# A fused attention and gated MLP on one core: one pair fetched per period, Erf behind the mean at a group's end, and means by two one-pass products

## The chip, the core and the metric

The kernel runs on one core of a Trainium2 chip. The metric is the device time of one execution, in microseconds (us). The engines are called as in the profile: PE is TensorE's matmuls and PEld its weight loads, DVE is VectorE, ACT is ScalarE, POOL is GpSimd, and SP is SyncE, which only issues transfers here.

## What is computed

The reference, cut to what matters (8 batches, 8 heads, 576 positions, 64 values per head; the MLP has 4608 rows, 512 in and out, 2048 hidden):

```python
kv = np.einsum('bhsd,bhse->bhde', k, v)            # per head, 64 x 64
out = np.einsum('bhsd,bhde->bhse', q, kv)
rms = np.sqrt(np.mean(out * out, axis=-1, keepdims=True) + 1e-06)
x = (out / rms * g_norm)                           # then (B,H,S,D) -> (B*S, H*D)

h = x @ w_in                                       # 4608 x 512 @ 512 x 2048
sp = np.maximum(h, 0.0) + np.log1p(np.exp(-np.abs(h)))
g = h * erf(sp)
return g @ w_out
```

## The kernel before

**Groups.** The rows are worked in nine groups of 512. Groups 0 to 7 are the first 512 positions of each batch, and group 8 (T == B in the code) collects the 64 positions left over of all eight batches. While the MLP of group T runs, the attention of group T + 1 is made, in four pairs of heads (p = 0 to 3).

**Number formats.** Group 0, the first two hidden tiles of group 1 and most of group 1's output layer multiply in fp32 (L907 for the hidden layer, L727 for the output). Elsewhere every factor is cut into forms of which each is multiplied in one pass: a high form, a low form, and one that combines both (`thirds`, with `upper` on ACT, L609, and `lower` on DVE, L612 and L615). A product of 128 x 512 then is twelve one-pass matmuls (L671): eight into the bank `n_ps`, four into `m_ps`. ACT empties `n_ps` (L1057) and DVE adds `m_ps` (L649). Six PSUM banks are used in turn as three pairs, so that a product needs the banks of the third product before it.

**Periods.** Groups 2 to 8 run in periods of a quarter of the hidden layer (four tiles of 128; the loop over m from L1007). A period has four hidden products (`hidden`), one after the other, with Softplus on each (L1072), then Erf on the four in two halves (L1078), then the four results (`result`, j = 0 to 3) of the period before. The gates `h * s` are multiplied on DVE (L1101), and the gated h is cut in its turn at the start of the next period.

**Attention of a pair, in pieces.** For groups 3 to 7 (`fused`) they are: `visit` (it multiplies q by kv, and turns q and makes k^T v for the pair after it), `halve` (the squares cut into a high and a low half, L521 and L522), `keep_tail` (copies out of PSUM), `loads` (the fetches of q, k and v of a later pair), `mean` (the products with the averaging matrix, L537 and L538 for halves or L543 in fp32, then Ln, Exp and Square on ACT, L552 to L554), `norm` (three DVE steps, L560 to L572) and `split` (into x's three forms). Mean squares are made in fp32 in groups 0, 1 and 8 and by halves in the others. `places` says behind which hidden product or result of the period a piece is put: at the last period of a group (b == NB - 1) `mean` is at place 5, behind the first result and behind Erf, `norm` at 6 and `split` at 7. A pair ahead of that is kept by `prepare` and `keep_prepared` in groups 1 and 2, whose pieces are put into the steps of groups 0 and 1 by `pieces_of`.

**What sets the order.** Each engine works through its own list in the order in which the code writes it. q, k and v of a pair lie in two buffers of each kind (`kvp`); the sync queue issues the fetches of pairs, the weights' parts (L809) and the stores in one order. Functions of ScalarE come in sets; a change of set is a table load (L105 for Ln and Exp, L108 for Softplus, L1078 for Erf's).

The lines that put the fetches in place, before:

```python
def loads():
    if not fused or (T, p) == (FIRST + 1, 0):
        load_pair(T * NP + p + 2)
    if fused:
        load_pair(T * NP + p + 3)
```

Of the kernel before, what the change touches and what calls it, by code (L numbers as in the profile page):

```python
# [54 lines left out]
FIRST = 2  # L55
# [5 lines left out]
def kernel(  # L61
# [10 lines left out]
    nc = tc.nc  # L72
# [320 lines left out]
    def keep_prepared():  # L393
        kept.pop()()

    def attention(T, p, pools=None):

        st = {}

        halves = FIRST <= T < B  # L400
        quad = 0 < T < B
        fused = FIRST < T < B
        then = divmod(T * NP + p + 1, NP)
# [55 lines left out]
        def visit():  # L459


            qT, tail = ready.pop((T, p))
            at = st["at"] = at_tile()
            x = halves_of(qT)
            for a, i, o in ((0, 0, 0), (0, 1, 1), (1, 0, 1), (1, 1, 0)):
                nc.tensor.matmul(  # L466
                    at[rows_of[o], a, 0 : 2 * P],
                    lhsT=bd[rows_of[i], a * D : a * D + D],
                    rhs=x[rows_of[i], a],
                    start=True,  # L470
                    stop=True,
                )
            for s in rows_of:
                nc.tensor.matmul(
                    at[s, 0, 2 * P : 2 * P + R], lhsT=bd[s, 0:D], rhs=tail[s], start=True, stop=True
                )
            st["o"] = at[:, :, 0 : 2 * P]
            st["next"] = fused and then[0] < B
            if st["next"]:
                ps = pair_of_banks("q0_ps", "q1_ps")  # L480
                kvs = list(kv_products(*then, at, crossed=True))
                turns = list(turn_products(*then, ps))
                while kvs or turns:
                    for some in (turns, kvs):
                        for product_ in some[:4]:
                            product_()  # L486
                        del some[:4]
            if fused:
                st["sq"] = x_new.tile([P, G], FP32, name="sq", tag="x")
            else:  # L490
                st["sq"] = qT
            nc.scalar.activation(two(st["sq"]), st["o"], AF.Square)
            if st["next"]:
                qT = turned(*then, ps)
                tails_kept(*then, ps, qT)

        def keep_tail():
            nc.vector.tensor_copy(
                out=x_last[:, p, T * R : T * R + R], in_=st["at"][:, 0, 2 * P : 2 * P + R]
            )  # L500
            if st["next"]:
                kv_kept(*then, st["at"])

        def apply():
# [53 lines left out]
        def norm():  # L558
# [19 lines left out]
                op1=ALU.mult,  # L578
            )

        def split():
            if T >= FIRST:
                thirds(st.pop("x"), *(form[:, p] for form in x_forms[T]))

        def loads():
            if not fused or (T, p) == (FIRST + 1, 0):
                load_pair(T * NP + p + 2)
            if fused:
                load_pair(T * NP + p + 3)

        if T == 0:
            return products, apply, halve, mean, norm
        if T == B:
            return lambda: None, square, lambda: None, mean, norm, split

        prepare_ = partial(prepare, T, p)
        if fused:
# [3 lines left out]
            pieces = ((prepare_,), (visit,), (halve, keep_tail, loads))  # L601
        else:
            pieces = ((prepare_, loads), (visit,), (keep_tail,))
        return (*(partial(chain, *group) for group in pieces), mean, norm, split)


    def upper(x, high):
# [20 lines left out]
    def thirds(x, high, low, both):  # L628
        upper(x, high)
        lower(x, high, low, both)  # L630
# [182 lines left out]
    def pieces_of(T):  # L813


        steps = [([], [], []) for _ in range(FC)]
        for p in range(NP):
            products, apply, halve, mean, norm, split = attention(T, p)
            f = (BATCH - 1) * (p + 1) if T < FIRST else BATCH * p

            steps[f][2 if T == FIRST or p == 1 else 1].append(products)
            steps[f + 1][0].append(keep_prepared)
            steps[f + 1][1].append(apply)
            steps[f + 2][0].append(halve)
            with_erf = (f + 2) % BATCH == BATCH - 1

            place = 2 if T < FIRST and p == 0 else 1
            steps[f + 2][place].append(partial(mean, table=not with_erf))
            steps[f + 3][0].append(norm)
            steps[min(f + 4, FC - 1)][0].append(split)  # L830
        return steps
# [27 lines left out]
    for n in range(FIRST * FC + 1):  # L859
# [10 lines left out]
        if T < FIRST:  # L870
            if f == 0:
                steps = pieces_of(T + 1)

            if due(0 if n == 2 * (BATCH - 1) else 1):
                weights()
            for key in list(w_new)[:2]:
                w_lower(*key)
            for piece in steps[f][0]:
                piece()
# [127 lines left out]
    for m in range(first_batch, batches + 1):  # L1007
        T, b = divmod(m, NB)
        todo = []
        if T + 1 < NG:  # L1010
            todo = list(attention(T + 1, b))
            if b == 0:
                side = late_r if T % 2 == FIRST % 2 else late
                forms = side.tile([P, 3, KC, G], FP32R, name=f"x_forms{(T + 1) % 2}")
                x_forms[T + 1] = [forms[:, i] for i in range(3)]

        def piece():
            if todo:
                todo.pop(0)()


        places = (0, 2, 3, 5, 6, 8)
        if T + 1 == B:
            places = (0, 0, 0, 5, 6, 7)
            if b == NB - 1:


                places, todo[3] = (0, 0, 0, 4, 6, 7), partial(todo[3], table=False)
                todo[5] = partial(chain, todo[5], softplus_table)
        elif b == NB - 1:  # L1030
            places = (0, 2, 3, 5, 6, 7)

        def pieces(place):
            while todo and places[-len(todo)] <= place:
                todo.pop(0)()

        def fetch(place):
            for which in FETCH[place].split():
                load_parts(which, 1)


        to_last = m == B * NB - 1
        pieces(0)
        g, done = g_next, len(g_next)
        g_next = []
        if m < batches:

            pool, tag = (acc, "e") if m % 2 else (wide, "b")
            h = pool.tile([P, BATCH, G], FP32, name="h", tag=tag)
            s = gate_r.tile([P, BATCH, G], FP32, name="s", tag="s")  # L1050
        for i in range(BATCH):
            if m < batches:
                n_ps, m_ps = hidden(T, b * BATCH + i)
            fetch(i)

            def evacuate():
                nc.scalar.activation(h[:, i], n_ps, AF.Copy, scale=SHIFT - 1.0)  # L1057
                add(h[:, i], m_ps)


            early_copy = i == 0 and m == B * NB
            if early_copy:
                evacuate()
            if i == 0:
                for half in range(done, 2):
                    g.append(cut_upper(old_h, half))
            if i == 0 and not done:
                cut_lower(old_h, 0, g[0])
            if m < batches:
                if not early_copy:  # L1070
                    evacuate()
                nc.scalar.activation(s[:, i], h[:, i], AF.Softplus)  # L1072
            if i == BATCH - 1:
                cut_lower(old_h, 1, g[1])
            pieces(i + 1)
        if m < batches:
            for i in range(2):
                nc.scalar.activation(part(s, i), part(s, i), AF.Erf)  # L1078
            if len(todo) < 2:
                softplus_table()  # L1080
        T2, b2 = divmod(m - 1, NB)
        w = [w_now["out", b2 * BATCH + f].pop(0).bitcast(FP32R) for f in range(BATCH)]
        for j in range(J):
            cuts = 2 if m == batches and j == J - 1 else 1
            result(T2, b2, j, g, w, cuts)
            fetch(BATCH + j)
            if b2 == NB - 1:
                e = es.pop(j)
                if cuts == 1:
                    store(T2, j, e)  # L1090
            if j == 1 and m == batches - 1:
                cut_lower(h, 0, g_next[0])

            if m >= batches - 1:
                due_halves = (j,) if j < 2 and m < batches else ()
            else:
                due_halves = range(2) if j == (2 if to_last else 1) else ()
            if to_last:
                pieces(BATCH + 1 + j)
            for half in due_halves:  # L1100
                nc.vector.tensor_tensor(  # L1101
                    out=part(h, half), in0=part(h, half), in1=part(s, half), op=ALU.mult
                )
            if j == 0 and m == batches - 1:
                g_next.append(cut_upper(h, 0))
            pieces(BATCH + 1 + j)
        old_h = h
# [33 lines left out]
```

## Time and profile before

| | before |
|---|---|
| time, median of 3 runs | 943.47 us (943.17 to 945.06) |
| span of the profiled execution | 943.4 us |
| granted TensorE clock, mean | 0.998 of full speed |
| PE busy | 920.1 us, 98% |
| DVE busy | 728.8 us, 77% |
| ACT busy | 603.1 us, 64% |
| DMA, mean over the span | 275 to 276 GB/s |
| groups 0 and 1 (to the first product of group 2) | about 254 us |
| one of groups 3 to 6 | about 98.7 us, four periods |

Busy shares are means over stages with different limits. A matmul's record reaches from its start to the modelled end of its pipeline, so that neighbouring records overlap and a busy PE isn't yet one at its peak. What a stage is bound by is read from the waits and from the spacing of its instructions. In a row of the timeline the first number is the start and the second the length in us; an idle stretch ahead and what ended it stand in brackets. Pieces of the chain of waits are start, us, what.

### The profile page before, as it was taken

What the parts mean: (1) busy time and instruction counts of PE and PEld (TensorE: products, weight loads), DVE (VectorE), ACT (ScalarE), POOL (GpSimd) and SP (SyncE); (2) the same over time, 40 slices, a digit from 0 to 9 for tenths busy, and PEclk for the clock granted to TensorE, in tenths of its full rate; (3) what the DMA queues carried; (4) which work ended last, traced back from release to release, by engine and by line L of the source; (5) the groups of instructions that cost most, each with busy time, mean ns of one, the idle gap of its engine ahead of it and who ended that gap; (6) DMA issues with size and microseconds to landing.
All of it is one profiled execution on the core that took longest, in us unless ns stands there. A gap on an engine that the chain in (4) does not pass through costs nothing.

```text
span 943.4 us, 15388 instructions
## 1 busy us (share of the span) xinstructions
PE 920.1 (98%) x5998; PEld 685.3 (73%) x5998; DVE 728.8 (77%) x1074; ACT 603.1 (64%) x830; POOL 2.4 (0%) x10
## 2 busy tenths in 40 slices
PE   6999999999999999999999999999999999999998
PEld 4444445565687887888788878887888788888886
DVE  2788848788576888888878887888888878776677
ACT  3877666677665666666656666666666666665552
POOL 1000000000000000000000000000000000000000
PEclk9999999999999999999999999999999999999999
DMA  9866406888589998899888988998877678778872
GB/s 258 287 209 205 135 1 253 322 342 333 200 288 333 330 335 296 289 321 329 272 296 311 320 290 303 333 309 278 284 318 261 247 264 342 275 281 324 321 271 56
DMA packets 108271, 259.99 MB, mean 276 GB/s; under 512 B 43992, under 2 KB 66856, under 8 KB 108200
## 3 DMA queue, kind: packets, MB, share of 16 engines
q1 hardware_dynamic: 106488, 256.73, 76.8%
q10 hardware_dynamic: 1648, 2.29, 0.8%
q8 instruction: 47, 0.77, 0.3%
q14 instruction: 24, 0.20, 0.1%
q0 software_dynamic: 64, 0.00, 0.0%
HBM read 224.40 MB, written 34.60 MB: 275 GB/s over the span
## 4 chain that ended last, share of the span: by engine, by line
PE 71%; DVE 16%; ACT 6%; DMA 4%; issue 2%; SPq 0%; DVEq 0%; ACTq 0%
PE n_ps L671 35%; PE m_ps L671 17%; PE o_ps L727 8%; PE h_ps L907 4%; DVE e L649 3%; DVE h L1101 2%; DVE e L644 2%; DVE h L649 2%; PE at_ps L466 1%; DVE g_forms L612 1%; DMA w_in_parts<-w_in 1%; PE at_ps L486 1%; DMA k_sb<-in_k_dram 1%; DVE x L572 1%; DVE u L563 1%
## 5 line engine op out<-in xcount | busy, mean ns | idle before, releaser
L671 PE MATMUL n_ps<-x_forms,w_in_parts 128*128 128x512 f32 x896 | 227.8, 395 | 6.2 <-DVE x_forms L612 3.9
L671 PE MATMUL n_ps<-w_out_parts,g_forms 128*128 128x512 f32 x928 | 232.0, 392 | 0.0
L671 PEld LDWEIGHTS n_ps<-w_out_parts,g_forms 128*128 128x128 f32 x928 | 172.9, 188 | 37.1 <-issue 1.9
L671 PEld LDWEIGHTS n_ps<-x_forms,w_in_parts 128*128 128x128 f32 x896 | 167.1, 188 | 45.0 <-DVE x_forms L612 5.6
L1072 ACT ACTIVATE s<-h 128x512 f32<-128x512 f32 x112 | 70.8, 632 | 190.4 <-DVE h L649 190.3
L649 DVE TENSOR_TENSOR h<-m_ps,h 128x512 f32<-128x512 f32 x116 | 79.9, 689 | 90.8 <-ACT h L1057 60.3
L671 PE MATMUL m_ps<-w_out_parts,g_forms 128*128 128x512 f32 (+1 forms) x468 | 124.3, 388 | 0.0
L671 PE MATMUL m_ps<-x_forms,w_in_parts 128*128 128x512 f32 x448 | 120.5, 391 | 0.0
L727 PE MATMUL o_ps<-w_out_sb,h_sb 128*128 128x512 f32 x224 | 101.8, 597 | 0.2 <-DVE h_sb L857 0.2
L671 PEld LDWEIGHTS m_ps<-w_out_parts,g_forms 128*128 128x128 f32 x468 | 87.5, 188 | 18.5
L671 PEld LDWEIGHTS m_ps<-x_forms,w_in_parts 128*128 128x128 f32 x448 | 84.7, 189 | 17.8
L649 DVE TENSOR_TENSOR e<-m_ps,e 128x512 f32<-128x512 f32 (+1 forms) x117 | 80.3, 687 | 14.5 <-PE m_ps L671 3.8
L727 PEld LDWEIGHTS o_ps<-w_out_sb,h_sb 128*128 128x128 f32 x224 | 41.4, 190 | 44.8 <-issue 42.2
L1057 ACT ACTIVATE h<-n_ps 128x512 f32<-128x512 f32 x112 | 66.1, 590 | 10.4 <-PE n_ps L671 10.2
L615 DVE SCALAR_TENSOR_TENSOR g_forms<-g_forms 128x1024 fp32r<-128x1024 f32 x58 | 71.1, 1225 | 2.0
L612 DVE TENSOR_TENSOR g_forms<-h,g_forms 128x1024 fp32r<-128x1024 f32 x58 | 70.5, 1216 | 0.1
L609 ACT ACTIVATE g_forms<-h 128x1024 fp32r<-128x1024 f32 x58 | 58.4, 1048 | 15.1 <-PE m_ps L671 11.1
L1101 DVE TENSOR_TENSOR h<-h,s 128x1024 f32<-128x1024 f32 x56 | 65.9, 1216 | 0.0
L907 PE MATMUL h_ps<-xT,w_in_sb 128*128 128x512 f32 x144 | 64.8, 596 | 0.5 <-DVE w_in_sb L245 0.5
L644 DVE SCALAR_TENSOR_TENSOR e<-n_ps,e 128x512 f32<-128x512 f32 x88 | 60.1, 683 | 3.5 <-PE n_ps L671 3.5
L108 ACT ACT_TABLE_LOAD x44 | 56.5, 1283 | 0.7
L1078 ACT ACTIVATE s<-s 128x1024 f32<-128x1024 f32 x56 | 56.3, 1053 | 0.3
(128 smaller groups left out, 1023.4 us busy)
## 6 DMA issues: line engine op xcount, KB each, us to landing
w_out_parts<-w_out SPq DMA_DIRECT2D x116, 768.0 KB
w_in_parts<-w_in SPq DMA_DIRECT2D x112, 768.0 KB
w_in<-w_new SPq DMA_DIRECT2D x16, 768.0 KB
q_sb<-in_q_dram SPq DMA_DIRECT2D x32, 256.0 KB
w_raw<-in_moe_w_in_dram SPq DMA_DIRECT2D x16, 512.0 KB
w_raw<-in_moe_w_out_dram SPq DMA_DIRECT2D x8, 1024.0 KB
out_dram<-e SPq DMA_DIRECT2D x32, 256.0 KB
k_sb<-in_k_dram SPq DMA_DIRECT2D x28, 287.5 KB
```

Of the source, the lines that this page charges most:

```text
L108: nc.scalar.preload_act_table_set("softplus")
L609: nc.scalar.activation(high, x, AF.Copy, scale=1.0 + 2.0**-13)
L612: nc.vector.tensor_tensor(out=low, in0=x, in1=high.bitcast(FP32), op=ALU.subtract)
L615: nc.vector.scalar_tensor_tensor(out=both, in0=low.bitcast(FP32), scalar=SHIFT, in1=high.bitcast(FP32), op0=ALU.mult, op1=ALU.add,)
L644: nc.vector.scalar_tensor_tensor(out=out_, in0=ps, scalar=scale, in1=out_, op0=ALU.mult, op1=ALU.add)
L649: nc.vector.tensor_tensor(out=out_, in0=ps, in1=out_, op=ALU.add)
L671: nc.tensor.matmul(ps[:, cols], lhsT=weights(form, k), rhs=moving(form, k)[:, cols], start=(form == forms[0] and k == 0), stop=(form == fo ...
L727: nc.tensor.matmul(o_ps[j], lhsT=g[:, j * P : j * P + P], rhs=w_out_sb[:, f, :], start=(f == 0), stop=last,)
L907: nc.tensor.matmul(plain[i], lhsT=w_in_sb[:, i % FC, c], rhs=xT[T][:, c, :], start=(c == 0), stop=(c == KC - 1),)
L1057: nc.scalar.activation(h[:, i], n_ps, AF.Copy, scale=SHIFT - 1.0)
L1072: nc.scalar.activation(s[:, i], h[:, i], AF.Softplus)
L1101: nc.vector.tensor_tensor(out=part(h, half), in0=part(h, half), in1=part(s, half), op=ALU.mult)
```

## The change

There are four edits, and none changes what is computed but for the rounding of the mean squares in two groups.

- **Fetches.** Every period fetches one pair, the second after its own. Before, the first fused period fetched two pairs and each later one the third after its own. For group 1 the fetches move from the step of `prepare` to the step of `keep_tail`.
- **The end of groups 2 to 6** (`turn`). The mean is put at place 4, behind the last hidden product, with its ACT steps ahead of Erf; norm and high form follow the first result, the low forms the second; Erf of the second half comes behind the first result; the gates move from the second to the third result. At the start of each group from 3 to 8 the first hidden product is copied out of PSUM ahead of the cut of the gated h (`early_copy`; before, in group 8 alone).
- **k^T v's copy.** In groups 0 and 1 `keep_prepared` runs at the top of a step, ahead of the weight cuts. In the fused visits the tails of the next pair are copied behind the halves.
- **Means.** Groups 1 and 8 cut the squares into halves and multiply these in one pass each.

```diff
-        halves = FIRST <= T < B
+        halves = 0 < T
...
             if st["next"]:
-                qT = turned(*then, ps)
-                tails_kept(*then, ps, qT)
+                st["turned"] = ps, turned(*then, ps)
...
-            if st["next"]:
+            if st.get("next"):
+                tails_kept(*then, *st.pop("turned"))
                 kv_kept(*then, st["at"])
...
+        def split_upper():
+            if T >= FIRST:
+                upper(st["x"], x_forms[T][0][:, p])
+
+        def split_lower():
+            if T >= FIRST:
+                lower(st.pop("x"), *(form[:, p] for form in x_forms[T]))
...
         def loads():
-            if not fused or (T, p) == (FIRST + 1, 0):
-                load_pair(T * NP + p + 2)
-            if fused:
-                load_pair(T * NP + p + 3)
+            load_pair(T * NP + p + 2)
...
         if T == B:
-            return lambda: None, square, lambda: None, mean, norm, split
+            return lambda: None, square, halve, mean, norm, split
...
-            steps[f + 1][0].append(keep_prepared)
             steps[f + 1][1].append(apply)
...
                 weights()
+            while kept:
+                keep_prepared()
             for key in list(w_new)[:2]:
                 w_lower(*key)
...
+        turn = b == NB - 1 and T + 1 < B
         if T + 1 < NG:
-            todo = list(attention(T + 1, b))
+            todo = list(attention(T + 1, b, in_parts=turn))
...
-        elif b == NB - 1:
-            places = (0, 2, 3, 5, 6, 7)
+        elif turn:
+            places, todo[3] = (0, 2, 3, 4, 5, 5, 6), partial(todo[3], table=False)
...
-            early_copy = i == 0 and m == B * NB
+            early_copy = i == 0 and b == 0 and first_batch < m < batches
...
-            for i in range(2):
+            for i in range(1 if turn else 2):
                 nc.scalar.activation(part(s, i), part(s, i), AF.Erf)
...
-                due_halves = range(2) if j == (2 if to_last else 1) else ()
-            if to_last:
+                due_halves = range(2) if j == (2 if to_last or turn else 1) else ()
+            if to_last or turn:
                 pieces(BATCH + 1 + j)
+            if turn and j == 0:
+                nc.scalar.activation(part(s, 1), part(s, 1), AF.Erf)
+                softplus_table()
```

More of the change, by code (lines that the diff above doesn't have):

```diff
@@ L394, in keep_prepared, with attention @@
         kept.pop()()
-    def attention(T, p, pools=None):
+    def attention(T, p, pools=None, in_parts=False):
         st = {}
-        halves = FIRST <= T < B
+        halves = 0 < T
         quad = 0 < T < B
@@ L579, in norm @@
             )
+        def split_upper():
[4 more added lines that the diff above has]
+                lower(st.pop("x"), *(form[:, p] for form in x_forms[T]))
         def split():
-            if T >= FIRST:
-                thirds(st.pop("x"), *(form[:, p] for form in x_forms[T]))
+            split_upper()
+            split_lower()
         def loads():
-            if not fused or (T, p) == (FIRST + 1, 0):
-                load_pair(T * NP + p + 2)
-            if fused:
-                load_pair(T * NP + p + 3)
+            load_pair(T * NP + p + 2)
         if T == 0:
@@ L603, in attention @@
             pieces = ((prepare_, loads), (visit,), (keep_tail,))
-        return (*(partial(chain, *group) for group in pieces), mean, norm, split)
+        after = (split_upper, split_lower) if in_parts else (split,)
+        return (*(partial(chain, *group) for group in pieces), mean, norm, *after)
     def upper(x, high):
```

## The prediction

> **What bounds the kernel now.** I read the page first, then the waits of TensorE (PE, and PEld for its weight loads), then the chain of waits and the timeline around each of these waits.
>
> ```profile
> PE 920.1 (98%) x5998; PEld 685.3 (73%) x5998; DVE 728.8 (77%) x1074; ACT 603.1 (64%) x830; POOL 2.4 (0%) x10
> ...
> PE 71%; DVE 16%; ACT 6%; DMA 4%; issue 2%; SPq 0%; DVEq 0%; ACTq 0%
> ```
>
> TensorE sets the pace: 71% of the chain. The 98% flatter it, since matmuls overlap; the pace is the spacing of the weight loads. A product of 12 one-pass matmuls takes 2.72 us from one product's first load to the next one's (352.43 to 355.15). What can be won is therefore TensorE's own work and the stretches in which this spacing breaks.
>
> ```profile
> PEld n_ps L671 <- DVE x_forms L612: 5.6, 5, 1.1
> ...
> PE n_ps L671 <- DMA w_in_parts<-w_in: 1.9, 1, 1.9
> ...
> PE at_ps L466 <- DVE bd_kv L364: 1.6, 1, 1.6
> ```
>
> Columns: us in total, times, longest. Three waits, and each has its own part in the change. The first comes at the start of a group. Its timeline:
>
> ```profile
> 453.38 1.32 PEld L671 LDWEIGHTS n_ps<-x_forms,w_in_parts 128*128 128x128 f32 x6
> ...
> 456.44 0.19 PEld L671 LDWEIGHTS n_ps<-x_forms,w_in_parts 128*128 128x128 f32 x1 [1.14 <-DVE x_forms L612]
> 456.55 0.90 PEld L671 LDWEIGHTS m_ps<-x_forms,w_in_parts 128*128 128x128 f32 x4
> 457.50 1.81 PEld L671 LDWEIGHTS n_ps<-x_forms,w_in_parts 128*128 128x128 f32 x8
> ```
>
> The first product of the group takes 457.50 - 453.38 = 4.12 us in place of 2.72. The low form of the last pair of x came late. Why, the chain of waits tells:
>
> ```profile
> 450.02 2.27 DVE h L1101 x2
> 452.29 0.61 DVE u L560
> 452.92 0.70 DVE u L563
> 453.65 0.75 DVE x L572
> ...
> 455.79 0.61 DVE x_forms L612
> ...
> 456.44 0.50 PE n_ps L671
> ```
>
> The gates (L1101) stand ahead of the norm in DVE's order, and a result's two additions between the norm and the split.
>
> The second wait stands alone, just after the main part begins; chain of waits again, then a row of the busy time by stretch:
>
> ```profile
> 270.32 8.44 DMA k_sb<-in_k_dram
> ...
> 279.26 11.45 DMA w_in_parts<-w_in
> 290.70 0.14 issue
> 290.84 3.14 PE n_ps L671 x8
> ```
>
> ```profile
> 291.60:295.00 3.40, 3.40 (x9) 2.65 (x8) 0.00 (x0) 1.22 (x2) 0.00 (x0) 0.50 1.06 407
> ```
>
> Weights fetched at 279.26 land at 290.70, behind the second of two pairs fetched in that period (its k was issued at 270.32). The 0.50 is the granted clock: after the stall TensorE runs at half speed for 3.4 us.
>
> **What the Trainium skill says.** "TensorE: Matmul & The Clock Gate", What's actually happening: the clock halves after an idle window of about 3.4 us and needs a busy one to come back. The 3.4 us at 0.50 agree; the loads stood only 2.32 us here, less than a window, and there the trace decides. The same page, Architectural detail: VectorE and ScalarE are strictly first in, first out. The chain above shows it: what stands ahead is waited for. "FP8 and Floating Point Precision", TensorE Precision Notes: true fp32 takes four passes. The trace has a 512-column fp32 product as two records, 0.86 us in all, against 0.226 us for a one-pass matmul: 3.8 times. "ScalarE: Activation LUTs", What ACT_TABLE_LOAD costs: about 1283 ns for every set; the trace has 1283 (L105, L108).
>
> **The change, part by part.**
>
> *One pair per period.* Each period after the first now fetches the next pair but one where it fetched the third; in all as many bytes. What goes is the second fetch at 269.6 to 275.9: 832 KB, at the 417 GB/s of 288.00 to 291.60 an estimated 2.0 us of transfer, and 6.4 us in which the sync queue held back the fetches behind it. The weights are due at 288.7, where TensorE would have begun, and landed at 290.7, so even the 2.0 us alone just suffice. Won: the product before the stall, 285.92 to 290.81, 4.89 - 2.72 = 2.17, and the one at half clock, 290.81 to 295.03, 4.22 - 2.72 = 1.50. Sum 3.7 us; at least 2. The shorter lead: a pair issued around 462 is read by the visit of the next period, near 485; the longest landing in the chain is 11.45 us. Hidden.
>
> *Group end.* In five periods (those that end groups 2 to 6) the mean's products go ahead of the first result, Ln, Exp and Square ahead of Erf, norm and split ahead of the gates. Table loads stay three. From the stamps of 440 to 458: Softplus ends at 445.5; table 1.28, Ln 0.69, Exp 0.63, Square 0.63: u at 448.8 (before: 452.2). DVE is free of the first result's additions at 448.6; norm 0.68 + 0.69 + 0.75 gives x at 451.0; ScalarE's high form 451.8, between the two Erfs (1.28 + 1.05 end at 451.1); the second result's additions to 452.4; low 453.1, both 453.8. TensorE wants high at 454.7, low at 455.0: no wait. The five first products took 3.62, 4.12, 4.11, 4.08 and 4.21 us: 20.14 - 5 x 2.72 = 6.5 us.
> The price: gates run at 455.2 to 457.5 where they ran at 449.9 to 452.3, and the last result's additions end at 458.9. Behind these in DVE's queue wait the new group's first addition and the cut of the gated h. The visit's banks must be free at 459.4 (0.5 us to spare), the third product wants the first one's bank at 460.5 and gets it at 459.6, because the early copy lets ScalarE empty it ahead of the cut. The fourth has 0.6 to spare. Group 7 has no visit, so there the third product comes 0.2 us too early. I take 6.3; both ends 3 and 6.9.
>
> *k^T v's copy.* In groups 0 and 1 it moves ahead of up to two weight cuts, 4 x 0.69 = 2.75 us. One visit waits: from n_ps at 170.8 to o_ps at 176.56 are 5.75 us, against 3.66 for the same stretch at 200.68. Two us are too much to count, for DVE is full there (11.71 of 12 us) and the next mean then waits for its halves, ready at 181.1 where TensorE could start at 180.8. I take 1.7, from 1.2 to 2.1. In the fused visits the tail copies move behind the halves: the mean's input comes about 0.5 us sooner, off the path.
>
> *Means of groups 1 and 8.*
>
> ```profile
> L522 DVE TENSOR_TENSOR sq_lo<-sq,sq_hi 128x512 fp32r<-128x512 f32 x20 | 13.8, 692 | 0.7
> ...
> L521 DVE CAST sq_hi<-sq 128x512 fp32r<-128x512 f32 x20 | 8.4, 422 | 13.0 <-ACT sq L492 13.0
> ...
> L543 PE MATMUL at_ps<-qT,mean_w 128*128 128x256 f32 x16 | 4.1, 379 | 0.0
> ...
> L543 PE MATMUL ms_ps<-sq,mean_w 128*128 128x512 f32 x8 | 4.1, 592 | 0.0
> ```
>
> Rows of the groups of instructions (busy us, mean ns): L543 on at_ps is group 1's mean, on ms_ps<-sq group 8's; L521 and L522 cut a square into halves.
>
> An fp32 mean holds TensorE 0.86 us in group 1 (chain, 75.45) and 0.89 in group 8 (828.98 to 829.43, and the n_ps after it 0.44 over its 1.81); by halves, 0.47 (four times 0.12, at 182.93) and 2 x 0.226. Saved 0.39 and 0.44 a pair. Added to DVE 0.42 + 0.69 = 1.11 us a pair. In group 8 it lies in DVE's gap before the period's first addition: 4 x 0.44 = 1.7 won. In group 1 three pairs have slack (the halves can be ready at 71.1, the mean comes at 75.3): 3 x 0.39 = 1.2. The first pair has none: from the square's end at 51.57 DVE's weight join runs to 55.67 and h_ps waits for it, so 1.1 are lost there. That group's fetches come two steps later, with four steps of about 7.8 us left: hidden.
>
> Sum: 3.7 + 6.3 + 1.7 + 1.7 + 1.2 - 1.1 = 13.5 us. 943.5 - 13.5 = **930.0 us**.
>
> **Rivals.**
> - The group end's wait comes back as a bank or DVE wait. For it: DVE has 77%, and the gates come 5 us later. Against: every margin above is positive. All of it lost: 936.3; half: 933.
> - The weights are late all the same, since the DMA share is 1.0 there: 930.0 + 3.7 = 933.7. Against: 2.0 to 6.4 us of room.
> - The halves of group 1 delay the weight joins in each of four pairs, no gain from the copy: 930.0 + 3 x 1.1 + 1.7 = 935.0. Against: one h_ps wait for a join after 40 us in the whole trace.
> - Slower: pairs fetched one period ahead come late. If each of the 19 visits of groups 3 to 7 that prepare another one waits 1 us and half of these drop the clock for 3.4 us (1.5 each), 19 + 14 = 33 are lost: 963. Against: 22 us of room.
>
> **How the numbers follow.** Forecast (within 2.5 of 930) 0.68, the first rival 0.12, second 0.07, third 0.05, slower 0.04, the parts cancelling 0.04. The three middle rivals are still faster by over 0.2% (1.9 us), so faster 0.92, same 0.04, slower 0.04. Range: all upper ends together (3.7 + 6.9 + 2.1 + 2.9, no loss) give 927.9, and a little more for spacing that the rows don't show, 926.5; above, the first rival at its worst, 936.5.
>
> **What would show it.** The five waits for x_forms gone and each group 2.72 us to its second product; no 0.50 clock near 292; the visit near 173 starting without a wait; L543 left with group 0 alone; a w_in_sb wait near 56 of 1 us more. Wrong would be: visits waiting for k_sb or v_sb, PE waiting on h or e (L649) after a group's start, or the weights' wait merely moved.

## The result and the profile after

| | before | after |
|---|---|---|
| time, median | 944.03 us (943.17 to 945.06, 4 runs) | 935.99 us (934.74 to 937.02, 4 runs) |
| span and time of the profiled execution | 943.4, 945.18 us | 935.2, 937.02 us |
| start of group 2's first product | 253.88 us | 255.95 us |
| from there to the end of the span | 689.5 us | 679.3 us |

The ratio after to before is 0.9914, with a 95% interval of 0.9894 to 0.9933: 8.0 us won, where 13.5 were forecast. The spans of the two profiles are 8.2 us apart. The last two rows say where to look: the periods of groups 2 to 8 gave 10.2 us, and groups 0 and 1 with their steps took 2.1 back.

The page after, its rows of busy time and of the chain of waits:

```profile
PE 916.1 (98%) x5998; PEld 683.8 (73%) x5998; DVE 736.2 (79%) x1090; ACT 603.4 (65%) x830; POOL 2.4 (0%) x10
...
PE 85%; DVE 9%; ACT 2%; DMA 2%; issue 1%; SPq 0%; DVEq 0%
```

TensorE now makes 85% of the chain in place of 71. The waits of TensorE after (us in total, times, longest):

```profile
PE h_ps L914 <- DVE w_in_sb L245: 1.9, 1, 1.9
...
PE at_ps L537 <- ACT w_new L639: 0.8, 1, 0.8
PE n_ps L677 <- DVE x_forms L618: 0.8, 1, 0.8
PE at_ps L537 <- DVE x_last L497: 0.5, 1, 0.5
```

All three waits that the change was aimed at are gone: for the weights (1.9), for k^T v's copy (1.6), and for x's low form at five group starts. The wait for `w_in_sb`, 0.5 us before, is now 1.9, and three others have come: ahead of two means, near 156 (0.5) and near 213 (0.8), and for x's low form at the start of group 8 (0.8, at 834). The weight loads at a group's start, timeline after, which answers to the one at 453.38 before:

```profile
450.50 1.77 PEld L677 LDWEIGHTS n_ps<-x_forms,w_in_parts 128*128 128x128 f32 x8
452.31 0.87 PEld L677 LDWEIGHTS m_ps<-x_forms,w_in_parts 128*128 128x128 f32 x4
453.22 1.77 PEld L677 LDWEIGHTS n_ps<-x_forms,w_in_parts 128*128 128x128 f32 x8
```

Eight loads and four without a break, and 2.72 us to the next product. All five group starts look so. The busy time by stretch (length, PE, PEld, DVE, ACT, POOL, granted clock, DMA share, GB/s), after:

```profile
57.00:59.00 2.00, 1.78 (x3) 0.84 (x4) 1.97 (x4) 1.97 (x3) 0.00 (x0) 0.72 0.90 290
59.00:60.50 1.50, 1.50 (x3) 0.66 (x2) 1.33 (x3) 0.96 (x1) 0.00 (x0) 0.50 1.04 368
60.50:62.60 2.10, 2.10 (x5) 0.87 (x5) 2.06 (x3) 0.00 (x0) 0.00 (x0) 0.81 0.48 119
291.60:295.00 3.40, 3.40 (x17) 2.82 (x16) 2.14 (x8) 1.12 (x2) 0.00 (x0) 1.00 0.92 316
```

The half clock near 292 is gone; one has come near 59, behind the wait of 1.9 us for `w_in_sb`. How many executions have either is taken up in the last section.

The two traces side by side. A stretch is measured from one product's first weight load to another's; "mean" is the product with the averaging matrix.

| part | stretch | before | after | difference | forecast |
|---|---|---|---|---|---|
| start | to the third mean of group 0 | 24.04 | 24.59 | +0.55 | 0 |
| first pair of group 1 | from there to that group's second mean | 50.82 | 53.47 | +2.65 | +1.1 |
| the other group 1 means | to its fourth mean | 47.65 | 46.87 | -0.78 | -0.8 |
| one more, and the copy | to group 2's first product | 131.37 | 131.02 | -0.35 | -0.4 - 1.7 |
| fetch | second period of group 2 | 28.44 | 24.40 | -4.04 | -3.7 |
| group ends | five first products | 20.14 | 13.60 | -6.54 | -6.3 |
| group 8's means | periods 28 (from its second product) to 32 | 109.69 | 110.12 | +0.43 | -1.7 |

The first row differs from run to run, since the first fetches set it. The two large terms came as forecast. Three small ones didn't: the first pair, the copy, and group 8.

### The profile page after: what moved, and what is told of

The parts are those of the page before. It is cut to its first block, busy times and chain, and to the rows that moved or that the text cites. A ratio compares the mean times of both kernels' runs of the same rounds, so it can differ in the third digit from the quotient of the medians.

```text
span 935.2 us, 15414 instructions
## 1 busy us (share of the span) xinstructions
PE 916.1 (98%) x5998; PEld 683.8 (73%) x5998; DVE 736.2 (79%) x1090; ACT 603.4 (65%) x830; POOL 2.4 (0%) x10
## 4 chain that ended last, share of the span: by engine, by line
PE 85%; DVE 9%; ACT 2%; DMA 2%; issue 1%; SPq 0%; DVEq 0%
PE n_ps L677 42%; PE m_ps L677 20%; PE o_ps L733 9%; PE h_ps L914 7%; PE at_ps L466 2%; PE at_ps L486 1%; DVE h L655 1%; DVE e L655 1%; PE q_ps L486 1%; DMA w_raw<-in_moe_w_in_dram 1%; DVE g_forms L618 1%; ACT s L1082 1%; PE at_ps L537 1%; DVE h L1114 1%; DVE e L650 1%
## 5 line engine op out<-in xcount | busy, mean ns | idle before, releaser
L677 PE MATMUL n_ps<-x_forms,w_in_parts 128*128 128x512 f32 x896 | 224.5, 392 | 1.0 <-DVE x_forms L618 0.8
L655 DVE TENSOR_TENSOR h<-m_ps,h 128x512 f32<-128x512 f32 x116 | 79.9, 689 | 79.8 <-ACT h L1067 58.5
L655 DVE TENSOR_TENSOR e<-m_ps,e 128x512 f32<-128x512 f32 (+1 forms) x117 | 80.4, 687 | 13.7 <-PE m_ps L677 2.7
L914 PEld LDWEIGHTS h_ps<-xT,w_in_sb 128*128 128x128 f32 x144 | 27.5, 194 | 35.5 <-issue 32.0
```

What stands on the lines that cost most here:

```text
L655: nc.vector.tensor_tensor(out=out_, in0=ps, in1=out_, op=ALU.add)
L677: nc.tensor.matmul(ps[:, cols], lhsT=weights(form, k), rhs=moving(form, k)[:, cols], start=(form == forms[0] and k == 0), stop=(form == fo ...
L914: nc.tensor.matmul(plain[i], lhsT=w_in_sb[:, i % FC, c], rhs=xT[T][:, c, :], start=(c == 0), stop=(c == KC - 1),)
```

## The experiments

All start from the changed kernel. Times are medians; the changed kernel's is 935.99 us. The medians of the kernel before that were taken beside the experiments lie between 943.25 and 943.65 us, and 944.03 beside the changed kernel, so that a difference of less than about 0.8 us between two medians is not read; there the traces decide.

**The first pair of group 1 in fp32**

```diff
-        halves = 0 < T
+        halves = 0 < T and (T, p) != (1, 0)
...
-        elif halves:
-            pieces = ((prepare_,), (visit,), (halve, keep_tail, loads))
+        elif 0 < T:
+            pieces = ((prepare_,), (visit,), ((halve,) if halves else ()) + (keep_tail, loads))
```

> The first pair of group 1 alone takes its mean in fp32 again, without the two cuts (L521, L522); its fetch stays where the change put it. Theory: the two cuts, 1.11 us of VectorE ahead of the weight join, are what makes the h_ps product near 57 wait 1.9 us for w_in_sb, and the wait makes the clock fall to 0.50 for 3.4 us behind it. Then the wait is 0.5 to 0.8 us again, no 0.50 clock near 57 to 62, h_ps takes 3.7 us instead of 5.4, and the first product of group 2 starts 2 to 3 us earlier (from 255.95 to about 253.5); time 2 to 3 us below the changed kernel's. Rival: the moved fetch of that pair is the cause; then wait, clock and time stay, plus 0.4 us for the fp32 mean.

Measured: 933.66 us (933.60 to 934.13), ratio to before 0.9895 (0.988 to 0.991); that is 2.3 us less. Group 2 starts at 252.68, and the wait for `w_in_sb` is 0.2 us. VectorE's rows of the timeline, the changed kernel first:

```profile
52.03 0.43 DVE L521 CAST sq_hi<-qT 128x512 fp32r<-128x512 f32 x1 [2.03 <-ACT qT L492]
52.49 0.69 DVE L522 TENSOR_TENSOR sq_lo<-qT,sq_hi 128x512 fp32r<-128x512 f32 x1
53.10 0.22 DVE L497 COPY x_last<-at_ps 128x64 f32<-128x64 f32 x1
53.23 0.68 DVE L232 TENSOR_SCALAR w_e<-w_raw 128x1024 f32<-128x1024 f32 x1
...
55.94 1.23 DVE L245 CUSTOM_DVE_ANT_0 w_in_sb<-w_e,w_m 128x2048 uint16<-128x2048 uint16 x1
```

and with this pair in fp32:

```profile
51.50 0.22 DVE L497 COPY x_last<-at_ps 128x64 f32<-128x64 f32 x1 [2.04 <-ACT qT L492]
51.64 0.68 DVE L232 TENSOR_SCALAR w_e<-w_raw 128x1024 f32<-128x1024 f32 x1
...
54.35 1.23 DVE L245 CUSTOM_DVE_ANT_0 w_in_sb<-w_e,w_m 128x2048 uint16<-128x2048 uint16 x1
```

The join (L232 to L245) puts the weights for `h_ps` together. From the square to the join's end the two cuts make the difference: 57.17 - 52.03 against 55.58 - 51.50, 1.06 us. The moved fetch is kept and the wait is gone, so the rival falls. The clock near 59 is 1.00 here.

**k^T v's copy back behind the weight cuts**

```diff
+            steps[f + 1][0].append(keep_prepared)
             steps[f + 1][1].append(apply)
...
-            while kept:
-                keep_prepared()
```

> The copy of k^T v goes back behind the weight cuts, all else as in the changed kernel. Theory: moved ahead, the copy takes 2 us from the visit near 173 and gives them back elsewhere, since it now waits at the head of VectorE's queue for ScalarE's qT with the cuts behind it, and the means near 156 and 213 wait. So with it moved back: o_ps waits 2 us near 173, no waits of over 0.6 us for the squares' halves near 156 and 213, and the time is within 0.7 us of the changed kernel's. Rival, the prediction's: the move brings 1.2 to 2.1 us net, so the time is 1.2 to 2.1 us longer.

Measured: 936.21 us (934.61 to 937.40), 0.2 us more than the changed kernel. The wait of 1.6 us for `bd_kv` is back, and those near 156 (0.5) and 213 (0.8) are gone. The move is worth nothing here. What it takes back, VectorE's timeline of the changed kernel shows:

```profile
145.16 0.36 DVE L358 COPY qT_last<-at_ps 128x64 f32<-128x64 f32 x2 [2.17 <-ACT qT L346]
145.43 0.28 DVE L364 TENSOR_REDUCE bd_kv<-at_ps 128x64 f32<-128x128 f32 x1
145.74 0.39 DVE L371 COPY bd_kv<-bd_kv 64x64 f32<-64x64 f32 x2
146.17 0.69 DVE L642 SCALAR_TENSOR_TENSOR w_new<-w_new,w_in_sb 128x512 fp32r<-128x512 f32 x1
...
154.36 0.42 DVE L521 CAST sq_hi<-qT 128x512 fp32r<-128x512 f32 x1
```

The copy at the head of the queue waits 2.17 us for ScalarE's turned q, and four weight cuts, ready long before, stand behind it. The Trainium skill, "TensorE: Matmul & The Clock Gate", Architectural detail, calls VectorE strictly first in, first out; this row shows its price. The work behind them moves back with them: the squares' halves end at 155.51 and the tail's copy out of the mean's bank (L497) at 155.65, right before the mean starts at 155.79. Near 213 it is the same (212.34, 212.48 and 212.62), though the list puts that wait down to ScalarE.

**The copy ahead for one pair alone**

```diff
+            steps[f + 1][0].append(lambda: kept and keep_prepared())
             steps[f + 1][1].append(apply)
...
-            while kept:
+            while kept and n == FC + 5:
                 keep_prepared()
```

> The copy of k^T v goes ahead of the weight cuts for the second pair of group 2 alone, the pair whose visit waited near 173 before; in all other pairs it stands where it stood. Theory: there nothing has to be waited for at the queue's head, so the 2 us of that visit are kept, less 0.3 at the next mean, and the waits of 0.9 to 1.3 us near 156 and 213 don't arise. From the first mean of group 1's last pair (near 125) to the first product of group 2's main part the span shortens by 1.4 to 1.9 us against the changed kernel, and the time by as much. Rival: what the copy saves is taken back anyway at the next mean, as VectorE is full there, and the time is within 0.5 us.

Measured: 934.20 us (932.93 to 934.91), 1.8 us less. Stretches from group 1's last mean over the four means of group 2 to the first product of the main part:

| copy | to 1st mean | to 2nd | to 3rd | to 4th | to the main part | sum |
|---|---|---|---|---|---|---|
| behind the cuts | 30.16 | 29.61 | 27.86 | 27.73 | 15.76 | 131.12 |
| ahead (the change) | 30.83 | 27.95 | 28.88 | 27.60 | 15.76 | 131.02 |
| ahead for the second pair | 30.16 | 28.06 | 27.73 | 27.73 | 15.75 | 129.43 |

The change wins 1.66 us in the second stretch and loses 0.67 and 1.02 in the first and third. Put ahead only where the copy's input is there by then, it keeps 1.7 us: what was forecast for the move as a whole.

**Group 8's means in fp32 again**

```diff
-        halves = 0 < T
+        halves = 0 < T < B
...
-            return lambda: None, square, halve, mean, norm, split
+            return lambda: None, square, halve if halves else lambda: None, mean, norm, split
```

> Group 8's four means in fp32 again, all else as in the changed kernel. Theory: the halves' 1.11 us stand ahead of the first addition and the cut of the gated h in VectorE's queue, and bring waits of TensorE for x_forms, e and h at the end; they cost about as much as the means save. So the last four periods of group 8's visits give back 0.43 us each, the last two periods lose their waits of 1.1 and 0.7 us, and the time is between 1.0 us shorter and 0.3 us longer. Rival, the prediction's: the halves lie in a gap and the four means bring 1.7 us, so the time is 1.7 us longer.

Measured: 935.67 us (934.23 to 936.54), 0.3 less. The periods take 22.66 four times and then 21.76 (112.40 in all), against 22.24, 22.24, 22.42, 23.13 and 22.81 (112.84) in the changed kernel: 0.44 us, and none of the waits for `x_forms` and `e` at the end. VectorE at a period's start, changed kernel:

```profile
791.56 0.42 DVE L521 CAST sq_hi<-sq 128x512 fp32r<-128x512 f32 x1
792.01 0.69 DVE L522 TENSOR_TENSOR sq_lo<-sq,sq_hi 128x512 fp32r<-128x512 f32 x1
792.62 1.22 DVE L618 TENSOR_TENSOR g_forms<-h,g_forms 128x1024 fp32r<-128x1024 f32 x1
793.87 1.23 DVE L621 SCALAR_TENSOR_TENSOR g_forms<-g_forms 128x1024 fp32r<-128x1024 f32 x1
795.02 0.69 DVE L655 TENSOR_TENSOR h<-m_ps,h 128x512 f32<-128x512 f32 x1
796.89 0.69 DVE L655 TENSOR_TENSOR h<-m_ps,h 128x512 f32<-128x512 f32 x1 [1.18 <-ACT h L1067]
```

No row ahead of the first addition (795.02) has an idle stretch. Nor has one in the trace of before, from which the prediction was made; there the idle stretch stands behind the first addition:

```profile
799.30 1.22 DVE L612 TENSOR_TENSOR g_forms<-h,g_forms 128x1024 fp32r<-128x1024 f32 x1
800.55 1.23 DVE L615 SCALAR_TENSOR_TENSOR g_forms<-g_forms 128x1024 fp32r<-128x1024 f32 x1
801.70 0.68 DVE L649 TENSOR_TENSOR h<-m_ps,h 128x512 f32<-128x512 f32 x1
803.56 0.69 DVE L649 TENSOR_TENSOR h<-m_ps,h 128x512 f32<-128x512 f32 x1 [1.19 <-ACT h L1057]
```

So the gap that the prediction put the halves into isn't there. And the delay isn't taken up again. The first addition of h after the start of each of the four periods, in us (starts from the rows of L655):

| | 28 | 29 | 30 | 31 |
|---|---|---|---|---|
| means in fp32 | 4.78 | 6.49 | 6.48 | 6.49 |
| halves first (the change) | 5.87 | 8.12 | 9.25 | 10.20 |
| halves in the gap (next) | 4.74 | 6.48 | 6.53 | 6.59 |

Against fp32 it is 1.1, 1.6, 2.8 and 3.7 us: it begins with the 1.1 us of the two cuts and grows with each period, and from the third one on TensorE waits for it.

**The halves in the gap**

```diff
-            places = (0, 0, 0, 5, 6, 7)
+            places = (0, 0, 2, 5, 6, 7)
...
-                places, todo[3] = (0, 0, 0, 4, 6, 7), partial(todo[3], table=False)
+                places, todo[3] = (0, 0, 2, 4, 6, 7), partial(todo[3], table=False)
```

> Group 8's squares are cut into halves after the second hidden product of a period in place of ahead of the first; the means stay one-pass. In the kernel with group 8's means in fp32 VectorE waits 1.18 us for ScalarE's copy three times per period between its additions, and the two cuts take 1.11 us. Theory: laid into such a gap they delay nothing, so all four periods take 22.24 us, and the waits for x_forms, e and h at the end vanish: 2.1 us shorter than the changed kernel, 1.7 shorter than group 8 in fp32. Rival: the halves come late for the mean or move the additions, and the periods stay at 22.4 us or more: at most 1 us shorter.

Measured: 932.76 us (932.49 to 933.72), ratio to before 0.9886 (0.9871 to 0.9901); 3.2 us less than the changed kernel. The four periods take 22.24 each and the next 21.76: 110.72, which is 2.12 us less. The rest of the 3.2 lies outside this stretch: this profile has no half clock near 59. VectorE there:

```profile
793.00 0.69 DVE L655 TENSOR_TENSOR h<-m_ps,h 128x512 f32<-128x512 f32 x1 [1.19 <-ACT h L1067]
793.61 0.42 DVE L521 CAST sq_hi<-sq 128x512 fp32r<-128x512 f32 x1
794.06 0.69 DVE L522 TENSOR_TENSOR sq_lo<-sq,sq_hi 128x512 fp32r<-128x512 f32 x1
794.88 0.69 DVE L655 TENSOR_TENSOR h<-m_ps,h 128x512 f32<-128x512 f32 x1
796.75 0.69 DVE L655 TENSOR_TENSOR h<-m_ps,h 128x512 f32<-128x512 f32 x1 [1.18 <-ACT h L1067]
```

An addition still starts each 1.88 us; the two cuts stand where VectorE waited for ScalarE's copy.

**Two pairs fetched at once**

```diff
-            load_pair(T * NP + p + 2)
+            if not fused or (T, p) == (FIRST + 1, 0):
+                load_pair(T * NP + p + 2)
+            if fused:
+                load_pair(T * NP + p + 3)
```

> The fetch goes back to two pairs in the first period of the main part and the third next one after it, all else as in the changed kernel. Theory: the second pair's transfer delays the weights of the first period, TensorE stalls about 2 us there and runs its next product at clock 0.50 for 3.4 us; the period takes 28.4 us in place of 24.4, and the time is 3.5 to 4.2 us longer. Rival: the fetch was late for another reason (the DMA engines are full there anyway), and the time stays within 0.7 us.

Measured: 937.79 us (937.27 to 938.85), 1.8 us more. In the trace the period takes 28.52 us in place of 24.40, with TensorE's wait for `w_in_parts` (1.9 us) and the clock at 0.50 behind it: 4.1 us. That profile has no half clock near 59, so that group 2 starts at 253.68, 2.3 us earlier than in the changed kernel's. The medians differ by less than the period does: the 3.5 to 4.2 us that were expected hold for the trace alone. The reading is in the last section.

**The group end undone, and the tail's copy**

The first of three kernels undoes the new group end and leaves the tail's copy behind the halves.

```diff
-        turn = b == NB - 1 and T + 1 < B
+        turn = False
...
-        elif turn:
-            places, todo[3] = (0, 2, 3, 4, 5, 5, 6), partial(todo[3], table=False)
+        elif b == NB - 1:
+            places = (0, 2, 3, 5, 6, 7)
```

> The group ends as before (both Erfs ahead of the mean's Ln, gates after the second result, the split in one piece), the early copy at a group's start kept, all else as in the changed kernel. Theory, the prediction's step: the group end is worth 6.3 to 6.6 us, and the first products of five groups take 3.6 to 4.2 us again, so the time is 6 to 7 us longer. Rival: part of the gain at the group ends came from the earlier fetch or from the early copy, and the time is at most 4 us longer.

Measured: 937.93 us (937.70 to 939.85), 1.9 us more, as the rival had it. The first products take 3.26 to 3.48 us and not 4.1, so that something which is still in place keeps part of the gain: the fetch, the early copy or the tail's place. Hence two more, one with the tail's copy first and the new end, and one with both old, which keeps the fetch and the early copy:

```diff
             if st["next"]:
-                st["turned"] = ps, turned(*then, ps)
+                qT = turned(*then, ps)
+                tails_kept(*then, ps, qT)
...
             if st.get("next"):
-                tails_kept(*then, *st.pop("turned"))
                 kv_kept(*then, st["at"])
```

> In the fused visits the copy of the turned tail (L358) goes back ahead of the squares' halves and of x_last, where it waits for ScalarE's turned q; the new group end stays, all else as in the changed kernel. Theory: e7 showed that the tail's place is worth 0.8 us at each old group end (first products 3.29 in place of 4.12); with the new group end the low form of x is ready about 3 us before TensorE wants it, so a chain 0.8 us later costs nothing there: first products stay at 2.72 and the time is within 0.7 us of the changed kernel's. Rival: the tail's place brings its 3.5 us whatever the group end, and the time is 3 us or more longer.

> Both go back: the tail's copy ahead of the halves and the group end as before; fetch, early copy and means stay as in the changed kernel. Theory: these two are all of the group end's 6.6 us, so the five first products take 3.6 to 4.2 us again, 6 to 7 us longer than the changed kernel in the trace's main part; time 941.5 to 943. Rival: the early copy or the fetch has a share, first products stay at 3.3 to 3.6 and the time is 2 to 4 us longer.

| tail's copy | group end | time, us | five first products, us | over 5 x 2.72 |
|---|---|---|---|---|
| first | old, kernel before | 944.03 | 3.62 4.12 4.11 4.08 4.21 | 6.54 |
| first | old | 941.56 (940.45 to 945.19) | 4.10 4.09 4.13 4.10 3.86 | 6.68 |
| behind | old | 937.93 | 3.29 3.29 3.29 3.26 3.48 | 3.01 |
| first | new | 935.65 (934.78 to 938.76) | 2.72 each | 0 |
| behind | new, the change | 935.99 | 2.72 each | 0 |

So it is the tail's place. It is worth 3.7 us with the old end and nothing with the new one; the new end is worth 6.7 alone and 3.0 on top by the first products (5.9 and 1.9 by the medians). The why, VectorE in a group's last period with the tail first (both old):

```profile
436.62 0.69 DVE L655 TENSOR_TENSOR h<-m_ps,h 128x512 f32<-128x512 f32 x1 [1.18 <-ACT h L1065]
438.75 0.50 DVE L358 COPY qT_last<-q_ps 128x64 f32<-128x64 f32 x2 [1.44 <-ACT qT L344]
439.17 0.42 DVE L521 CAST sq_hi<-sq 128x512 fp32r<-128x512 f32 x1
...
441.10 0.69 DVE L655 TENSOR_TENSOR h<-m_ps,h 128x512 f32<-128x512 f32 x1
```

and with the tail behind the halves (old end):

```profile
433.33 0.69 DVE L655 TENSOR_TENSOR h<-m_ps,h 128x512 f32<-128x512 f32 x1 [1.18 <-ACT h L1065]
435.20 0.43 DVE L521 CAST sq_hi<-sq 128x512 fp32r<-128x512 f32 x1 [1.18 <-ACT sq L492]
...
437.41 0.69 DVE L655 TENSOR_TENSOR h<-m_ps,h 128x512 f32<-128x512 f32 x1
```

The copy waits 1.44 us for the turned q, with the halves and the third addition behind it. From the second addition to the third are 4.48 us in place of 4.08, and the delay of the period ahead adds to these 0.4: in a group's last period the third addition starts 13.28 us after the period's start in place of 12.47 and the mean's Ln 21.15 in place of 20.34, 0.8 us later.

**No early copy**

```diff
-            early_copy = i == 0 and b == 0 and first_batch < m < batches
+            early_copy = i == 0 and m == B * NB
```

> At a group's start ScalarE again cuts the gated h first and copies the new group's first product after it; all else as in the changed kernel. The prediction's step: the gates end 3.3 us into the new group, the cut takes ScalarE 2.0 us and the copy comes behind it, so the third product of the group finds its bank late, 0.2 to 1 us in each of five groups: 1 to 5 us longer. Rival: VectorE's first addition then ends some 8.5 us into the group and the bank is wanted at 9.3, so nothing waits: within 0.5 us.

Measured: 940.07 us (938.48 to 940.99), 4.1 us more, but not at the third product, which starts on time in every group (2.72 us and, where a visit lies between, 4.77 or 4.78). Without the early copy the first addition comes 7.4 us into group 4 in place of 4.6, and the delay stays through the group and grows over the groups: 6.95, 7.42, 8.27, 7.93 and 8.49 at five starts. TensorE meets it elsewhere, at means that wait for the tail's copy out of their bank, as at the end of group 6:

```profile
731.53 0.36 PE L537 MATMUL at_ps<-sq_hi,mean_w 128*128 128x256 f32 x1 [0.88 <-DVE x_last L497]
```

The main part is 3.4 us longer in the trace: 1.1 in that period, 1.5 in two periods that have group 8's halves as well, and most of the rest in group 5. How much of the 1.5 belongs to the early copy alone was not tested.

**The three findings together**

fp32 for the first pair of group 1, the copy ahead for the second pair of group 2 alone, and group 8's halves in the gap, with the edits shown above.

> The three findings together: the first pair of group 1 in fp32 (2.3 us), the copy ahead for the second pair of group 2 alone (1.4 to 1.9), group 8's halves in VectorE's gap (2.1). Theory: the three lie in stretches apart, so they add up to 5.5 to 6.3 us under the changed kernel: 929.5 to 930.5. Rival: the savings in groups 0 and 1 are taken back where the main part starts (its weights or forms come later than TensorE), and the time is 931.5 or more.

Measured: 930.82 us (930.12 to 931.66), ratio to before 0.9865 (0.9848 to 0.9881). That is 5.2 us under the changed kernel's median, a little less than expected; the spans of the two profiles are 6.4 apart: 2.3 in the stretch of the first pair, 1.6 in group 2's, 2.1 in group 8 and 0.5 at the start. For `w_in_sb` TensorE waits 1.0 us here, where the first experiment had 0.2; what makes this difference isn't shown. Its page:

```profile
PE 912.6 (98%) x5998; PEld 683.7 (74%) x5998; DVE 735.0 (79%) x1088; ACT 602.8 (65%) x830; POOL 2.4 (0%) x10
...
PE 93%; ACT 3%; DMA 2%; DVE 1%; issue 0%; SPq 0%; DVEq 0%; ACTq 0%
```

It beats both kernels, with the fetch and the group end of the change.

## Why the prediction was right and where it failed

The time lies in the range that was given (926.5 to 936.5 us), half a microsecond from its upper end, and not within 2.5 us of 930, which had a chance of 0.68. That end was set by the first rival at its worst, which did not come; that other misses add up to less is luck. Nor does the number say which theory held: the first rival's 936.3 and the third's 935.0 lie nearer to 935.99 than the forecast does. The traces do.

*The bound* was read rightly: TensorE's spacing, broken at three places; each break that the change aimed at is gone, and the time fell.

*One pair per period*, forecast 3.7 us: 4.0 in the traces, the stall and the half clock behind it. The second rival, weights late all the same, is out. No visit waits for k or v, so the slower rival found nothing. In the medians the fetch is worth 1.8. What was mis-sized is the half clock, put at 1.5 us: the profile of before has it, and most executions have not. It shows in the mean granted clock of an execution: the 3.4 us at half take 0.0018 off it, and the profile of before has 0.998; of the 39 executions of that kernel beside the experiments 37 have 0.999 or 1.0.

*Group end*, forecast 6.3: 6.5, and no wait of the first rival's kind. The sum was right and two reasons were wrong. The tail's copies were put down as "off the path". With the old end they were on it and made over half of the loss (3.7 of 6.7 us); with the new one they are off it. The early copy was to save the third product's bank. It does save 4 us, but by keeping an addition chain that has no slack from falling behind.

*k^T v's copy*, forecast 1.7: 0.1. The failed step is "one visit waits": only what stands behind the cuts was counted, and not that the copy at the head of the queue would wait for ScalarE in its turn, with the cuts behind it. The wait for the visit went, and two waits for means came. On this point the third rival (no gain from the copy) was right, but not on group 1's means, below.

*Group 8*, forecast -1.7: +0.4. The failed step is "it lies in DVE's gap before the period's first addition". There is no such gap, in the trace of before either; there is one of 1.18 us between additions, and laid there the two cuts cost nothing and the four means bring their 1.7.

*Group 1*: three means saved 0.39 us each, as forecast. The first pair was to lose 1.1. Between group 1's first two means, where before took 21.14 us, the six kernels with the same cuts and no half clock near 59 take 21.8 to 22.7, so that they lose 0.7 to 1.5; the one whose wait is nearest to the changed kernel's loses 22.24 - 21.14 = 1.1. The term left out is the half clock behind the wait: in the profile of the changed kernel the stretch takes 23.81, another 1.6 us. The prediction had counted just this effect at 292 and not looked for it at the one wait that it forecast itself.

The misses: 1.6 for the copy, 2.1 for group 8, 1.6 for the clock and 0.55 for the start, less 0.6 that fetch and group ends brought over. They make the 5.3 us by which the two profiles' spans, 8.2 us apart, fall short of the forecast. The profile of before has a half clock that was forecast to go and went, that of the changed kernel one that wasn't forecast. For executions without either, as most are by their mean clocks, the 1.5 us forecast for the half clock at 292 take the place of the 1.6 near 59; 1.5, 1.6 for the copy and 2.1 for group 8 make an estimated 5.2 of the 5.5 us between the medians.

With these three parts placed differently the kernel takes 930.8 us. That this is the forecast's number is in part chance: with the first pair in fp32 the 1.1 us that it was to lose go too, and the prediction's own sum would be 928.9.

## What to carry to other kernels

An instruction moved ahead is only early if its own inputs are there: ask for each move what the moved one waits for and what then stands behind it, for the engine's queue pays for both. Work "in a gap" needs the gap's row: look for the idle stretch in the timeline of that very place, and if the engine runs in a chain without slack, count the delay once per period and not once. And where a forecast has a new stall of TensorE in it, the clock behind the stall belongs to the sum, weighted by how often it falls: a half clock in one profile need not be in the median, and the mean clocks of the other executions tell.

## What was not expected of the hardware

Nine more kernels have the two cuts ahead of the same join. Their profiles show a wait of TensorE for `w_in_sb` near 57, and the stretch between the first two means of group 1:

| wait, us | 1.9 | 1.9 | 3.0 | 2.2 | 1.6 | 2.0 | 2.5 | 1.6 | 1.6 | 1.6 |
|---|---|---|---|---|---|---|---|---|---|---|
| kernel | changed | fp32 in group 8 | tails first | both old | copy back | two pairs | copy for one pair | halves in gap | old end | no early copy |
| clock below 0.7 near 59 | yes | yes | yes | yes | no | no | no | no | no | no |
| stretch, us | 23.8 | 23.8 | 24.6 | 24.1 | 21.8 | 22.2 | 22.7 | 21.8 | 21.8 | 21.8 |

After a stall of 1.9 us the clock stood at half for 3.4 us, and after one of 2.5 it didn't: the length of the stall doesn't settle it, and what does isn't shown by these runs. With the half clock the stretch is about 1.4 to 2 us longer.

How often it comes is read from the mean clocks. Of the changed kernel's four executions 937.02, the one that was profiled, has 0.998. The other three (936.96, 935.02 and 934.74) have 0.999, which leaves no room for 3.4 us at half; so the clock explains at most one of the two longest, and what made the other isn't shown. The kernel with tail and group end both old ran 20 times: six executions have 0.995 to 0.998 and take 942.61 to 945.19 us, fourteen have 0.999 or 1.0 and take 940.45 to 942.09. There the lower clock and the longer time go together, 2.5 us between the two averages, though only one of them was profiled, so that the place of the low clock in the others isn't known.

It bears on the fetch in the same way. With two pairs at once the profiled execution, which has the half clock near 292, has a mean clock of 0.998 and is the longest of the four (938.85); the other three have 0.999 or 1.0 and take 937.27 to 938.07. So the 4.1 us of the trace hold for one of the four executions, and the median has 1.8.
